# A fused gradient kernel on one core: first branch loads in two parts, a row tile placed by hand, loads at the half change reordered, the last step's sums moved up

## The chip, the cores and the metric

The kernel runs on one core of a Trainium2 chip. The metric is the time of one execution on the device in microseconds (us), the median of several. A ratio is computed as the mean time of one kernel's fast runs over the mean of the other's fast runs in the same rounds, so it is not quite the ratio of the medians that stand beside it.

A profile is one execution, traced. Executions of one kernel lay up to 7 us apart (1928.34 to 1935.41 in one group). Each kernel was traced once; as far as the traces of kernels with the same start tell, such differences come from when transfers land in the first 60 us, and from whether the clock falls after a wait, but this is inferred. A wait in a trace is therefore read as a mechanism, and the time as a ratio with its interval.

## The reference

It is the gradient of a layer norm that feeds two branches: a long convolution with a four-tap shift (branch A) and a gated two-layer network (branch B). Cut to what matters:

```python
xn = _layernorm(A_q)                      # S = 2048 rows, D = 1024
# branch A: k_shift = four taps of k by shift_k; kv = k_shift * v
#           y = irfft(rfft(kv) * rfft(ssm_k)) + kv * ssm_D;   a = xn * y
# branch B: gate = relu(xn @ W_gate); h = gate * (xn @ W_up);  b = h @ W_down   (F = 3584)
out = A_q + a + b
# returned: out and the gradients of q, k, v, shift_k, ssm_k, ssm_D, W_gate, W_up, W_down
```

## The kernel before

The program text is written once, and its order on each engine is then set by priorities and by ties. `keep_in_program_order` ties an instruction to the one of the same engine that was emitted just before it. `now()` and `late()` set the priority of what follows; what is late and not tied is placed wherever the queue has nothing more urgent.

```python
class Pri:
    LATE = 100_000_000
    def now(self):
        self.n += 64
        self.tc.cur_priority = self.n
    def late(self):
        self.n += 64
        self.tc.cur_priority = self.n + self.LATE
...
    def load(self, out, in_):                      # branch A's loads
        self.pri.now()
        ins = self.nc.sync.dma_start(out=out, in_=in_)
        if self.pin:
            self.tc.keep_in_program_order(ins)
        else:
            self.pri.pin(ins)

    def store(self, out, in_):                     # branch A's stores
        self.pri.late()
        self.pri.pin(self.nc.sync.dma_start(out=out, in_=in_))
```

The four taps of the shift go through a small array in memory, `sk_d`: transposed on TensorE, copied by ScalarE, stored, and later loaded again, one copy for each partition (`skb`). In the kernel before:

```python
    def shift_rows(self):
        ...
        self.act(sk_t[:], ps[:])
        self.store(self.sk_d, sk_t[:])
...
        self.shift_rows()
        self.pin = True
        nx = self.loads_1(0)      # hn, gt, xt, sD
        self.loads_2(nx)          # kp, vt, skb
        self.pin = False
        yield 11000
```

Branch B is computed in 7 blocks of 512 columns, for two halves of 8 row tiles each. In the first block the row tiles come straight from the layer norm, which works in chunks (0 to 3 of one row tile, 4 and later of two). Per chunk, ScalarE makes two row sums, VectorE averages them, ScalarE takes a square root, VectorE scales. TensorE then flips the row tile (`pst_x`), VectorE copies it (`xnT`), and the products with the gate weights (`wg`, result `ps_g`), the up weights (`wu`, `ps_u`) and the down weights (`wdT` with `goT`, `ps_h`) follow. VectorE turns each `ps_u` into `ru` and so frees its accumulator. Branch A runs beside this in 8 groups of 128 columns. Its work is cut into steps, each with a piece for TensorE and a piece for the other engines; an empty step has none for TensorE.

```python
            for sp in range(0, HS, 2):
                self.pri.now()
                while len(gT) < min(sp + 6, HS):
                    gT.append(self.load_T(g, len(gT), "goT", HS + len(gT)))
                ...
                yield from grad(sp)
                if ahead:
                    with self.tc.issue_after(self.stored.ins):
                        load(6 + sp // 2)          # rows of the layer norm's chunk 6, 7, ...
```

At the half change the second half's `xnT` and `goT` are loaded by transposing transfers between the next weights. `while late` and `late` in the diff below concern these. The last step, per row tile, is the gradient through the layer norm:

```python
            for ob in range(2):                    # two halves of 512 columns
                ... 56 matmuls into ps ...
                V.tensor_tensor_reduce(out=gx[:, oc], in0=ps[:], in1=gy[:, oc], ... accum_out=m[:, ob:ob + 1])
                V.tensor_tensor_reduce(out=pr[:, oc], in0=gx[:, oc], in1=xn[:, oc], ... accum_out=m[:, 2 + ob:3 + ob])
            ... three small operations on m ...
            for ob in range(2):
                nc.scalar.activation(out=w[:, oc], in_=xn[:, oc], ... scale=m[:, 5:6], bias=m[:, 4:5])
                V.scalar_tensor_tensor(out=gx[:, oc], in0=gx[:, oc], scalar=rstd, in1=gt[:, oc], ...)   # multiply-add
                V.tensor_tensor(out=o1[:, oc], in0=gx[:, oc], in1=w[:, oc], op=ALU.add)
                nc.sync.dma_start(out=out1[rows, oc], in_=o1[:, oc])
```

## Time and profile before

| | kernel before |
|---|---|
| time, median of 3 | 1940.89 us (1940.74 to 1941.39) |
| TensorE busy | 1891.5 us, 98% of the span |
| TensorE idle, 0 to 120 us | 16.4 us |
| granted clock of TensorE, 100 to 120 us | 0.83 |
| granted clock, 20 to 40, 40 to 60 and 120 to 140 us | 1.00 |

TensorE is the bound, so only its waits count, plus the stretches in which it ran at a lower clock. The prediction shows the lines.

### The profile page before, as it was taken

Reading aid. Unit: us, or ns where it says so; the run is one execution under the profiler, and the core shown is the slowest. Engines: PE = TensorE matmul, PEld = TensorE weight load, DVE = VectorE, ACT = ScalarE, POOL = GpSimd, SP = SyncE. Lnnn points to the kernel's source line nnn. Section 1 sums busy time; section 2 is a strip of 40 time slices with the busy share of each in tenths; the row PEclk is TensorE's granted clock in tenths of the full one; section 3 lists DMA queues with packets and bytes.
Section 4 is the critical chain, followed back from the end, with each engine's and each line's share of the span. In section 5 each row is a group of like instructions: output and inputs, shape, how many; then the busy total and the mean of one; then the engine's idle time right before and its main releaser. Section 6 shows DMA issues by size and latency. Waiting matters only on the chain.

```text
span 1938.3 us, 35924 instructions
## 1 busy us (share of the span) xinstructions
PE 1891.5 (98%) x15294; PEld 881.5 (45%) x15526; DVE 910.2 (47%) x1378; ACT 630.3 (33%) x863; POOL 15.3 (1%) x38
## 2 busy tenths in 40 slices
PE   8989999999999999999999999999999999999998
PEld 3434444444444444444444444444444444444443
DVE  6677777777686664444444344310122222222222
ACT  5555355355455444344344344311000000000000
POOL 1000000000000000000000000000000000000000
PEclk9999999999999999999999999999999999999999
DMA  9794887985775883654753643384999854554451
GB/s 252 233 196 131 179 186 172 212 200 131 180 186 132 217 244 107 151 149 141 197 148 106 145 123 121 99 233 178 259 238 245 204 134 121 120 121 122 118 121 36
DMA packets 616017, 319.08 MB, mean 165 GB/s; under 512 B 450984, under 2 KB 585136, under 8 KB 615856
## 3 DMA queue, kind: packets, MB, share of 16 engines
q1 hardware_dynamic: 605360, 295.79, 62.1%
q10 hardware_dynamic: 9216, 16.78, 2.8%
q0 software_dynamic: 1280, 4.20, 0.7%
q8 instruction: 121, 1.98, 0.4%
q14 instruction: 40, 0.33, 0.1%
HBM read 141.56 MB, written 95.44 MB: 122 GB/s over the span
## 4 chain that ended last, share of the span: by engine, by line
PE 66%; issue 2%; DMA 0%; DVE 0%; ACT 0%
PE ps_w L1032 19%; PE ps_x L1214 19%; PE ps_o L1180 10%; PE ps_d L1032 8%; PE ps L72 4%; PE ps_h L795 1%; PE ps_u L795 1%; PE ps_d L1045 1%; PE ps_g L795 1%; PE ps_w L1045 1%; DMA ugs<-ug_d 0%; PE pst L304 0%; DMA xn_nat<-xn_d 0%; DVE flp L315 0%; DVE o L1230 0%
## 5 line engine op out<-in xcount | busy, mean ns | idle before, releaser
L1032 PE MATMUL ps_w<-ugs,xn_nat 128*128 128x512 bf16 x1672 | 376.6, 379 | 5.3 <-issue 3.5
L795 PEld LDWEIGHTS <-xnT 128*128 128x128 bf16 x1792 | 170.5, 98 | 222.9 <-issue 13.0
L1032 PEld LDWEIGHTS <-xn_nat 128*128 128x128 bf16 x1728 | 165.0, 98 | 199.3 <-issue 5.5
L795 PE MATMUL ps_g<-wg,xnT 128*128 128x512 bf16 x868 | 205.6, 382 | 15.9 <-DMA wg<-in_B_W_gate_dram 9.3
L1227 ACT ACTIVATE w<-xn,m 128x512 f32<-128x512 bf16 x32 | 24.3, 806 | 559.5 <-issue 317.2
L795 PE MATMUL ps_h<-wdT,goT 128*128 128x512 bf16 x863 | 202.9, 379 | 3.3 <-issue 1.3
L795 PE MATMUL ps_u<-wu,xnT 128*128 128x512 bf16 x867 | 203.3, 379 | 2.3 <-issue 1.3
L1214 PE MATMUL ps_x<-wuT,guT 128*128 128x512 bf16 x879 | 197.6, 379 | 0.9
L1214 PE MATMUL ps_x<-wgT,ggT 128*128 128x512 bf16 x878 | 197.3, 379 | 0.9
L1180 PE MATMUL ps_o<-wd,hT 128*128 128x512 bf16 x878 | 192.6, 379 | 0.9
L1032 PE MATMUL ps_d<-g_nat,hs 128*128 128x512 bf16 x740 | 167.7, 379 | 3.3 <-issue 2.7
L1180 PEld LDWEIGHTS <-hT 128*128 128x128 bf16 x896 | 87.7, 98 | 105.7
L1214 PEld LDWEIGHTS <-guT 128*128 128x128 bf16 x896 | 87.7, 98 | 105.7
L1214 PEld LDWEIGHTS <-ggT 128*128 128x128 bf16 x896 | 87.7, 98 | 105.7
L895 DVE SCALAR_TENSOR_TENSOR ru<-ru,ps_u 128x512 bf16<-128x512 bf16 x112 | 76.6, 684 | 120.9 <-issue 48.6
L315 DVE STREAM_TRANSPOSE flp<-C 128x1024 f32<-128x1024 f32 x48 | 90.6, 1933 | 89.2 <-ACT C L76 89.2
L795 PEld LDWEIGHTS <-goT 128*128 128x128 bf16 x896 | 85.2, 98 | 103.3 <-issue 3.7
L1216 DVE CUSTOM_DVE_ANT_0 gx<-ps_x,gy 128x512 f32<-128x512 f32 x32 | 22.1, 692 | 215.2 <-PE ps_x L1214 205.4
L952 ACT CAST gh<-ps_h 128x512 bf16<-128x512 f32 x112 | 65.6, 585 | 169.6 <-PE ps_h L795 158.7
L76 ACT CAST C<-ps 128x1024 bf16<-128x1024 f32 x96 | 92.5, 1015 | 74.4 <-PE ps L72 73.4
L1130 ACT CAST wi<-ps_w 128x512 bf16<-128x512 f32 x108 | 63.7, 590 | 154.7 <-PE ps_w L1032 150.0
L315 DVE STREAM_TRANSPOSE flp<-B 128x1024 f32<-128x1024 f32 x48 | 90.8, 1938 | 47.8 <-ACT B L76 47.8
(169 smaller groups left out, 1517.3 us busy)
## 6 DMA issues: line engine op xcount, KB each, us to landing
ug_d<-ru SPq DMA_DIRECT2D x112, 256.0 KB, 3.3
ugs<-ug_d SPq DMA_DIRECT2D x112, 256.0 KB, 4.4
wg<-in_B_W_gate_dram SPq DMA_DIRECT2D x56, 256.0 KB, 4.3
wu<-in_B_W_up_dram SPq DMA_DIRECT2D x56, 256.0 KB, 5.8
h_d<-ht SPq DMA_DIRECT2D x112, 128.0 KB, 4.2
hs<-h_d SPq DMA_DIRECT2D x56, 256.0 KB, 5.1
out_dram<-wi SPq DMA_DIRECT2D x56, 256.0 KB, 2.8
gt<-in_grad_out_dram SPq DMA_DIRECT2D x32, 256.0 KB, 4.2
```

The lines of the kernel that those rows point to most:

```text
L72: self.pri.pin(self.nc.tensor.matmul(out, lhsT=lhsT, rhs=rhs, start=start, stop=stop))
L76: self.pri.pin(self.nc.scalar.copy(out=out, in_=in_))
L315: self.pri.pin(self.nc.vector.transpose(out=df[:, c0:c0 + 32, :], in_=sf[:, c0:c0 + 32, :]))
L795: self.pri.pin(self.nc.tensor.matmul(ps[:], lhsT=xT[:, kt * P:(kt + 1) * P], rhs=w(kt), start=(kt == 0), stop=(kt == self.DT - 1)), always ...
L895: self.pri.pin(nc.vector.scalar_tensor_tensor(out=ru[s][:, 1, :], in0=ru[s][:, 0, :], scalar=0.0, in1=ps[:], op0=ALU.is_gt, op1=ALU.mult))
L952: self.pri.pin(nc.scalar.copy(out=gh[:], in_=ps[:]))
L1032: self.pri.pin(self.nc.tensor.matmul(ps[:], lhsT=lhsT(st), rhs=rhs(st), start=(st == 0), stop=(st == self.ST - 1)))
L1045: self.pri.pin(self.nc.tensor.matmul(ps[i][:], lhsT=lhsT(i, st), rhs=rhs(i, st), start=(st == 0), stop=(st == self.ST - 1)))
L1130: self.pri.pin(nc.scalar.copy(out=wo[0][:, d, :], in_=ps[:]))
L1180: nc.tensor.matmul(ps[:], lhsT=hT[:, kt, :], rhs=self.wd[:, kt, oc], start=(kt == 0), stop=(kt == self.FT - 1))
L1214: nc.tensor.matmul(ps[:], lhsT=T[:, kt, :], rhs=W[:, kt, oc], start=(i == 0), stop=(i == n - 1))
L1227: nc.scalar.activation(out=w[:, oc], in_=xn[:, oc], func=ACT.Identity, scale=m[:, 5:6], bias=m[:, 4:5])
```

## The change

Its intent, part by part: (1) issue those of the branch's first loads that depend on nothing earlier, so that the gate weights of the third block are not stuck behind them; (2) take chunk 4 of the layer norm out of the way of the fourth row tile; (3) put two transposing loads of the half change behind the weights; (4) in the last step, make the small sums before the second multiply-add; (5) move one empty step ahead of the second transform of K. The core of the diff:

```diff
@@ loads_1, loads_2: xt (reads xn_d) and skb (reads sk_d) leave them
-        xt = self.xp.tile([P, 16, P], BF16, name="xt")
-        self.load_time(xt, self.xn_d, cg)
+    def load_xn(self, st):  ...
+    def load_taps(self, st):  ...
@@ start of the branch
-        self.shift_rows()
         self.pin = True
         nx = self.loads_1(0)
         self.loads_2(nx)
+        yield 12000
+        self.shift_rows()
+        yield 11000
+        self.load_xn(nx)
+        self.load_taps(nx)
         self.pin = False
-        yield 11000
+        yield 9000
...
-A_START = 66_000
+A_START = 45_000
@@ second transform of K
         yield None, q
+        yield None, q
         f2K = self.fwd2(st, "K", "fK")
         yield f2K, q
         yield None, q
         yield f2K, q
-        yield None, q
@@ first block of branch B: chunk 4
+                if sp == 2:
+                    chunk()
                 up(sp)
...
                 yield from first_gate_up(0)
-                chunk()
                 yield from first_gate_up(2)
@@ half change
                 if end:
                     load_up()
+                while end and late:
+                    late.pop(0)()
...
-                            ngT.append(self.load_T(g, HS + s, "goT", HS + s))
+                            late.append(lambda s=s: ngT.append(self.load_T(g, HS + s, "goT", HS + s)))
+                    while late and sp != HS - 4:
+                        late.pop(0)()
@@ last step: the first half's multiply-add at once, the three small operations tied, then
             for ob in range(2):
                 nc.scalar.activation(out=w[:, oc], ...)
+                if ob:
+                    hd(V.scalar_tensor_tensor(out=gx[:, oc], ...))
                 V.tensor_tensor(out=o1[:, oc], in0=gx[:, oc], in1=w[:, oc], op=ALU.add)
```

More of the change, by code (lines that the diff above doesn't have):

```diff
@@ L260, in loads_1, with load_xn @@
         self.load_time(gt, self.g, cg)
-        xt = self.xp.tile([P, 16, P], BF16, name="xt")
-        self.load_time(xt, self.xn_d, cg)
         sD = self.sm.tile([P, P], BF16, name="sD")
         self.load(sD[:], self.ssm_D[cg].partition_broadcast(P))
-        return dict(gi=gi, cg=cg, hn=hn, gt=gt, xt=xt, sD=sD)
+        return dict(gi=gi, cg=cg, hn=hn, gt=gt, sD=sD)
+    def load_xn(self, st):
+        xt = st["xt"] = self.xp.tile([P, 16, P], BF16, name="xt")
+        self.load_time(xt, self.xn_d, st["cg"])
     def gate_grad(self, st):
@@ L280, in loads_2, with load_taps @@
         self.load_time(vt, self.v, cg)
-        skb = self.sm.tile([P, 4, 1, P], BF16, name="skb")
+        st["kp"], st["vt"] = kp, vt
+    def load_taps(self, st):
+        skb = st["skb"] = self.sm.tile([P, 4, 1, P], BF16, name="skb")
         self.load(skb[:].rearrange("p i o c -> p (i o c)"),
                   self.sk_d[4 * st["gi"]:4 * st["gi"] + 4, :].rearrange("i c -> (i c)").partition_broadcast(P))
-        st["kp"], st["vt"], st["skb"] = kp, vt, skb
     def taps(self, st, out, src, offs):
@@ L499, in next_1 @@
                 st["nx"] = self.loads_1(gi + 1)
+                self.load_xn(st["nx"])
         def next_2():
@@ L503, in next_2 @@
                 self.loads_2(st["nx"])
+                self.load_taps(st["nx"])
         def next_gate():
@@ L858, in hidden @@
             nb = (n + 1) % self.FB
-            ru, nw = {}, [None, None, None]
+            ru, nw, late = {}, [None, None, None], []
             def load_gate():
@@ L1219, in grad_x @@
                                        op0=ALU.mult, op1=ALU.add, accum_out=m[:, 2 + ob:3 + ob])
-            V.tensor_tensor(out=m[:, 4:6], in0=m[:, 0:4].rearrange("p (a b) -> p a b", b=2)[:, :, 0],
-                            in1=m[:, 0:4].rearrange("p (a b) -> p a b", b=2)[:, :, 1], op=ALU.add)
-            V.tensor_scalar(out=m[:, 6:8], in0=m[:, 4:6], scalar1=-1.0 / D, scalar2=None, op0=ALU.mult)
-            V.tensor_scalar(out=m[:, 4:6], in0=m[:, 6:8], scalar1=self.rstd[:, st:st + 1], scalar2=None, op0=ALU.mult)
+                if ob == 0:
+                    self.tc.keep_in_program_order(V.scalar_tensor_tensor(
+                        out=gx[:, oc], in0=gx[:, oc], scalar=self.rstd[:, st:st + 1], in1=gt[:, oc], op0=ALU.mult,
+                        op1=ALU.add))
+            hd = self.tc.keep_in_program_order
+            hd(V.tensor_tensor(out=m[:, 4:6], in0=m[:, 0:4].rearrange("p (a b) -> p a b", b=2)[:, :, 0],
+                               in1=m[:, 0:4].rearrange("p (a b) -> p a b", b=2)[:, :, 1], op=ALU.add))
+            hd(V.tensor_scalar(out=m[:, 6:8], in0=m[:, 4:6], scalar1=-1.0 / D, scalar2=None, op0=ALU.mult))
+            hd(V.tensor_scalar(out=m[:, 4:6], in0=m[:, 6:8], scalar1=self.rstd[:, st:st + 1], scalar2=None,
+                               op0=ALU.mult))
             o1 = p_ev.tile([P, D], BF16, name="o1")
@@ L1227, in grad_x @@
                 nc.scalar.activation(out=w[:, oc], in_=xn[:, oc], func=ACT.Identity, scale=m[:, 5:6], bias=m[:, 4:5])
-                V.scalar_tensor_tensor(out=gx[:, oc], in0=gx[:, oc], scalar=self.rstd[:, st:st + 1], in1=gt[:, oc],
-                                       op0=ALU.mult, op1=ALU.add)
+                if ob:
+                    hd(V.scalar_tensor_tensor(out=gx[:, oc], in0=gx[:, oc], scalar=self.rstd[:, st:st + 1],
+                                              in1=gt[:, oc], op0=ALU.mult, op1=ALU.add))
                 V.tensor_tensor(out=o1[:, oc], in0=gx[:, oc], in1=w[:, oc], op=ALU.add)
```

## The prediction

> **What bounds the kernel now.** I read, in this order, the busy times of the page, the busy time per stretch of the span, the list of waits of TensorE, and then the timelines around the few waits that it names.
>
> ```profile
> PE 1891.5 (98%) x15294; PEld 881.5 (45%) x15526; DVE 910.2 (47%) x1378; ACT 630.3 (33%) x863; POOL 15.3 (1%) x38
> ```
>
> TensorE (PE) is the bound: 1938.3 - 1891.5 = 46.8 us is all that it does not work. The change removes no matmul, so it can only give back part of these 46.8 us plus what a throttled clock costs. Faster by 2% would need 38.8 us. The view by stretches says where the idle time is: 16.4 us in the first 120 us (4.6 of them between 20 and 40, 8.1 between 100 and 120), 2.5 us between 320 and 360, 7.5 us after 1900, and otherwise 0.3 to 2 us per 100 us. The list of TensorE's waits (total us, times, longest) gives the early ones names:
>
> ```profile
> PE ps_g L795 <- DMA wg<-in_B_W_gate_dram: 9.3, 3, 7.3
> PE ps_g L795 <- DVE xnT L827: 3.9, 3, 2.9
> ...
> PE pst_x L824 <- DVE ln_x L776: 1.8, 2, 1.6
> ...
> PE ps L72 <- DVE flp L315: 1.5, 3, 0.8
> ```
>
> In the timeline of TensorE (start, length, what, and in brackets the idle time before it with its releaser) the single cases are:
>
> ```profile
> 22.18 0.62 PE L824 MATMUL pst_x<-ident,ln_x 128*128 128x128 bf16 x8 [1.63 <-DVE ln_x L776]
> ...
> 27.39 1.90 PE L795 MATMUL ps_g<-wg,xnT 128*128 128x512 bf16 x8 [2.87 <-DVE xnT L827]
> ...
> 113.96 3.59 PE L795 MATMUL ps_g<-wg,xnT 128*128 128x512 bf16 x8 [7.30 <-DMA wg<-in_B_W_gate_dram]
> ...
> 357.39 1.24 PE L795 MATMUL ps_g<-wg,xnT 128*128 128x512 bf16 x4 [0.53 <-DMA wg<-in_B_W_gate_dram]
> 360.06 3.03 PE L795 MATMUL ps_g<-wg,xnT 128*128 128x512 bf16 x12 [1.43 <-DMA wg<-in_B_W_gate_dram]
> ```
>
> The longest is explained by the sync queue's own timeline before it. The queue issues in order, and it stood still from 91.7 to 98.1 us:
>
> ```profile
> 90.31 1.42 SPq L88 DMA_DIRECT2D gt<-in_grad_out_dram  x2
> 98.12 1.31 SPq L88 DMA_DIRECT2D xt<-xn_d  x2
> 99.48 1.19 SPq L88 DMA_DIRECT2D sD<-in_A_ssm_D_dram  x1
> 100.72 3.60 SPq L88 DMA_DIRECT2D kp<-in_A_k_dram  x4
> 104.36 1.83 SPq L88 DMA_DIRECT2D vt<-in_A_v_dram  x2
> 106.24 1.58 SPq L88 DMA_DIRECT2D skb<-sk_d  x1
> ...
> 108.39 1.26 SPq L957 DMA_DIRECT2D ug_d<-ru  x2
> 109.74 2.22 SPq L788 DMA_DIRECT2D wg<-in_B_W_gate_dram  x4
> ```
>
> The load of xt reads xn_d, whose last rows GpSimd stores at 91.9 to 93.0; they land some 5 us later (5.0 us is the median landing of these stores). Behind it sD, kp, vt and skb take 8.3 us of issuing, and only then come the gate weights that TensorE wants at 106.66. At the very end of the kernel, the timeline of VectorE and ScalarE shows the last row tile:
>
> ```profile
> 1932.09 0.16 DVE L1220 TENSOR_TENSOR m<-m 128x2 f32<-128x2 f32 x1
> 1932.17 0.74 DVE L1228 SCALAR_TENSOR_TENSOR gx<-gx,rstd,gt 128x512 f32<-128x512 f32 x1
> 1932.83 0.16 DVE L1222 TENSOR_SCALAR m<-m 128x2 f32<-128x2 f32 x1
> 1933.03 0.23 DVE L1223 TENSOR_SCALAR m<-m,rstd 128x2 f32<-128x2 f32 x1
> 1933.34 1.52 ACT L1227 ACTIVATE w<-xn,m 128x512 f32<-128x512 bf16 x2 [22.66 <-issue]
> ```
>
> A 0.74 us multiply-add stands between the small sums that the activation waits for.
>
> **What the Trainium skill says.** First, "TensorE: Matmul & The Clock Gate", section "What's actually happening": after an idle window of about 3.4 us the clock falls to half until TensorE has been busy for such a window. The trace agrees: after the 7.30 us wait the granted clock from 113.96 to 117.35 is 0.50, and these matmuls last up to 634 ns where the group's median is 379. Second, the same page, section "Architectural detail": VectorE and ScalarE take their instructions strictly in order. The trace fits: the copy of xnT that TensorE waited for at 27.39 ran on VectorE at 26.66, directly behind the layer norm of a later chunk. Third, "Perfetto Trace Analysis", section "DMA Instruction — HWDGE (DVE, Sync)": an issuing sequencer first waits for the semaphore, then holds the descriptor generator, and only then takes the next instruction. That is the standstill before xt at 98.12. Fourth, "DMA: Bandwidth & Descriptors", section "Issuing engines are not separate DMA queues": all transfers share 16 engines. It matters for the first 60 us, where the trace's DMA share is 1.03 to 1.06.
>
> **The change part by part.**
>
> Part 1, loads in two parts. hn, gt, sD, kp and vt move about 12 TensorE steps (12 x 1.73 = 21 us) earlier, to about 65 us; xt and skb stay near 90; the start of the branch does not move (66 + 11 against 45 + 12 + 11 + 9, both 77 in the pacing's units). The last xn_d store does not get later, so xt is issued at 98.1 again (every time here is on the old scale), skb at 99.4, the two ug_d stores at 101.1, and wg at about 102.4: 7.3 us sooner. In the old trace TensorE began 113.96 - 109.74 = 4.2 us after the first wg issue; 102.4 + 4.2 = 106.6, and TensorE wants it at 106.66. So the 7.30 us wait goes nearly whole. I keep 0.3 us, as four tiles issued over 2.2 us may trail. The throttle goes with it: from 113.96 to 118.20 the clock was half, so 4.24 / 2 = 2.1 us, plus 0.1 us at the next group (2.02 against 1.89). Sum: 7.3 + 2.2 - 0.3 = **9.2 us**. Can VectorE follow? In the new order the branch's gate product starts when it did (104.7), and the taps follow at about 106.9 in place of 111.75; the flip is then done at about 118.6, where the second transform is reached at 130.07 - 9.2 = 120.9. It holds, with some 2 us left.
>
> Part 2, the fourth row tile. Taking chunk 4 of the layer norm out of the way of chunk 3: between 18.5 and 21.6 VectorE did 1.3 us of chunk 4's work, and ScalarE's square root waited for a row sum (1.04 us). I put the fourth tile at 21.3 instead of 22.18, so TensorE's 1.63 us wait shrinks by about 0.9; its copy then comes right behind, at about 22.7, before the multiply by up-weights ends at 23.6, so the 2.87 us wait vanishes. Gain to there: about 3.8 us. But chunk 4 now starts its sums at about 21, where it was 17.8, and took 8 us; its tiles are ready at 29 to 30, and TensorE, running 3.8 us ahead, wants them at 32.58 - 3.8 = 28.8. I give back 0.8 us: **3.0 us**. Chunk 5 (done at 39.5) is wanted at 43.93 - 3.0 = 40.9, fine.
>
> Part 3, the half change. In the old queue two goT transposes were issued at 348.86 and held it for 4.31 us; the gate weights went out at 353.94. Their buffer was free when the last gate product ended, at about 348.6. With the transposes behind both weights, wg goes out some 4 to 5 us sooner, and 0.53 + 1.43 = **2.0 us** go. The late tiles are used over 20 us later.
>
> Part 4, the last step. Without the 0.74 us instruction, the two small ones follow 0.2 us apart and the activation starts at about 1932.8 in place of 1933.34: **0.5 us**. In the other 15 row tiles VectorE is idle 7 to 10 us per half, so there it is worth nothing.
>
> Part 5, one empty step moved before the second transform of K, in each of eight groups. The wait for the flip arose three times, 0.78 + 0.34 + 0.42 = 1.5 us, and a step is 1.7 us long, so it should go. The product that reads K has one step less; VectorE waits there, but has had idle steps behind. I count **1.2 us**.
>
> Sum: 9.2 + 3.0 + 2.0 + 0.5 + 1.2 = 15.9 us. 1940.9 - 15.9 = 1925.0; I add 0.5 us for small new waits and predict **1925.5 us**, a ratio of 0.992.
>
> **The rivals.**
>
> A: the wait moves. xn_d still bounds xt, and xt still stands ahead of the weights. If the stores land later (their landing runs up to 8.2 us), or if the earlier 2 MB of loads push the stores and weight transposes of the stage at 65 to 75 us back, then wg comes 2 to 4 us later than I say. For it: the standstill of 6.4 us remains in the queue. Against it: hn and gt no longer fly beside the last xn_d store, and from 70 to 90 the DMA share is only 0.35 to 0.53. Result: 1928 to 1930, or up to 1932 when the wait passes 3.4 us and throttles again.
>
> B: the start is bound by transfers. The DMA share is over 1 until 60 us, so a TensorE that runs 3 us ahead might meet inputs not landed (goT, the weights of the second block). Against it: in the old trace TensorE has no wait for a DMA there; the second block's gate weights were issued at 52.0 to 54.7 and wanted at 61.5. Result: part 2 worth 0 to 1 us, 1927.5 to 1928.5.
>
> C: everything goes, chunk 4 is ready in time too: 9.5 + 4.5 + 2.0 + 0.5 + 1.5 = 18.0, so 1923.
>
> **Range and chances.** C is nearly the floor, 1922.5 with rounding; A in its bad form with a part of B sets the upper end, 1932. Faster by 2% would be under 1902, which 46.8 us of idle time, most of it in start, end and gaps of 0.16 us, cannot give. Slower by 2% would take a race of waits that no part introduces; all transfers moved are moved earlier, or behind something more urgent.
>
> **What would show it.** Right: the wait for wg near 106 us gone or under 1 us and the clock 1.00 from 100 to 120; wg issued straight behind xt, skb and two ug_d stores; no wait for xnT at the fourth tile, and one of about 1 us at the fifth; no wg wait at the half change; the last activation 2.2 us after the last product's first sum starts, where it was 2.7 (1930.62 to 1933.34). Wrong: a wait of over 2 us for wg in front of the third block, a new wait on goT or wdT before 60 us, or TensorE waiting for VectorE in the first group of the branch.

## More of the kernel before

The kernel before was run again beside each group of experiments; its medians lie between 1939.95 and 1941.35 us, so every experiment is read by its ratio to the runs of before of its own group.

The sync queue's timeline (start, time in the queue, line, transfer, count) has the store of the taps well before anybody wants them:

```profile
88.97 0.34 SPq L96 DMA_DIRECT2D sk_d<-sk_t  x1
```

## The result, and the profile after

The changed kernel took 1938.76 us (median of 4, 1937.82 to 1940.31) beside 1940.82 us (median of 4) of the kernel before. The ratio is 0.999, with a 95% interval of 0.9972 to 1.0007: the same within 2%, as foretold, but the gain is about 2 us where 15.4 were predicted, and the time is outside the range.

The list of waits of TensorE after (total us, times, longest us) has lost the wait for the gate weights, 9.3 us before, and has got others:

```profile
PE pst_x L834 <- DVE ln_x L786: 5.5, 3, 4.5
...
PE ps L72 <- DVE flp L319: 3.2, 1, 3.2
...
PE ps_h L805 <- DMA wdT<-in_B_W_down_dram: 1.4, 1, 1.4
...
PE ps_d L1060 <- ACT wo L1112: 0.8, 1, 0.8
```

In the timeline of TensorE after (idle time and its releaser in brackets):

```profile
33.92 1.30 PE L834 MATMUL pst_x<-ident,ln_x 128*128 128x128 bf16 x16 [4.54 <-DVE ln_x L786]
...
108.67 1.89 PE L805 MATMUL ps_g<-wg,xnT 128*128 128x512 bf16 x8
...
122.50 1.89 PE L805 MATMUL ps_g<-wg,xnT 128*128 128x512 bf16 x8 [1.59 <-DVE ru L905]
127.61 1.06 PE L72 MATMUL ps<-flp,FW 64*32 64x128 bf16 x64 [3.23 <-DVE flp L319]
...
145.60 0.60 PE L72 MATMUL ps<-kvt,R 64*128 64x512 bf16 x4
...
366.05 0.59 PE L805 MATMUL ps_h<-wdT,goT 128*128 128x512 bf16 x2 [1.42 <-DMA wdT<-in_B_W_down_dram]
```

The third block's gate product starts at 108.67 with no wait, where it started at 113.96 after 7.30 us: 5.3 us ahead. But by 127.61 TensorE has waited 1.59 + 3.23 us for VectorE, and the throttle follows: the view by stretches gives a granted clock of 0.83 between 120 and 140, where before it had 0.83 between 100 and 120. The product on kvt, which reads what the taps produce, starts at 145.60. In the kernel before:

```profile
145.30 0.60 PE L72 MATMUL ps<-kvt,R 64*128 64x512 bf16 x4
```

So all of the lead is gone within 37 us. Every later row of the comparison is small. Cut at three milestones of TensorE's timeline (differences of starts; the last column is the span; `ps_d` holds products of the gradient of W_down, `ps_o` those of branch B's output):

| kernel | to kvt | kvt to first ps_d | ps_d to first ps_o | ps_o to the end | span |
|---|---|---|---|---|---|
| before | 145.30 | 548.00 | 656.96 | 588.04 | 1938.3 |
| after | 145.60 | 545.41 | 658.11 | 588.28 | 1937.4 |

The first column holds parts 1 and 2, the second parts 3 and 5, the third another piece of part 5, and the last part 4. Three of the four columns are longer after the change.

**Where the lead went.** The sync queue's timeline after:

```profile
97.27 1.37 SPq L88 DMA_DIRECT2D xt<-xn_d  x2
...
100.34 2.40 SPq L798 DMA_DIRECT2D wg<-in_B_W_gate_dram  x4
...
109.51 0.59 SPq L96 DMA_DIRECT2D sk_d<-sk_t  x1
113.03 0.33 SPq L88 DMA_DIRECT2D skb<-sk_d  x1
```

The gate weights are issued at 100.34, even earlier than the 102.4 of the prediction. But the store of the taps, issued at 88.97 before, is now issued at 109.51, although ScalarE had made `sk_t` at 80.12; and `skb`, which the prediction put at 99.4, has to wait for it until 113.03. The cause stands in the two program texts. The store is late by priority. In the kernel before, the next instruction of its queue was a pinned load, and a pin ties the load to the store: the store could go no later than the load. The change moved the loads ahead of `shift_rows`, so nothing follows the store that is tied to it, and it sank behind everything urgent. VectorE's timeline after shows the price:

```profile
115.94 1.23 DVE L80 TENSOR_TENSOR ksh<-kp,skb 128x2048 bf16<-128x2048 bf16 x1 [6.92 <-DMA skb<-sk_d]
```

In the kernel before this first tap started at 111.75. All taps, the multiplies that free the accumulators (`ru`) and the flip (`flp`) are in one engine's order, and so TensorE waited for two of them.

**The start.** ScalarE's timeline after:

```profile
30.91 1.06 ACT L742 ACTIVATE ln_j<-ln_x 128x1024 bf16<-128x1024 bf16 x1 [3.44 <-DMA ln_x<-in_A_q_dram]
...
31.96 0.19 ACT L774 ACTIVATE ln_s<-ln_s 128x2 f32<-128x2 f32 x1
```

The 0.19 us square root of chunk 4 stands behind the first row sum of chunk 5 (VectorE had its input ready at 27.60), and that sum waits for chunk 5's rows to land. In the kernel before the same root ran ahead of that sum, at 23.90:

```profile
23.90 0.20 ACT L764 ACTIVATE ln_s<-ln_s 128x2 f32<-128x2 f32 x1 [0.65 <-DVE ln_s L763]
```

The fourth row tile gained nearly what was foretold (the gate product behind it starts at 24.04 in place of 27.39, with no wait), and the fifth lost it: a wait of 4.54 us, and a clock of 0.91 from 20 to 40. The second block's first gate product starts at 63.30, where it was 61.52 before.

**The half change.** The gate weights are issued at 349.62 in place of 353.94 and nothing waits for them. But the displaced transposes, of which two hold the queue for 4.54 us, still stand ahead of the last piece of the down weights:

```profile
355.20 4.54 SPq L822 DMA_TRANSPOSE goT<-in_grad_out_dram  x2
```

That piece goes out at 362.49, where it went out at 363.87 before: 1.4 us sooner. TensorE begins the product that needs it at 363.18 in place of 366.38, 3.2 us sooner, and so it now waits 1.42 us inside it.

**The last step.** VectorE's timeline of the last row tile after:

```profile
1932.50 0.69 DVE L1252 TENSOR_TENSOR o<-gx,w 128x512 bf16<-128x512 f32 x1 [0.93 <-ACT w L1248]
1933.11 0.75 DVE L1250 SCALAR_TENSOR_TENSOR gx<-gx,rstd,gt 128x512 f32<-128x512 f32 x1
1933.96 0.69 DVE L1252 TENSOR_TENSOR o<-gx,w 128x512 bf16<-128x512 f32 x1
```

In the kernel before, the lines that the prediction shows were followed by both output sums at once:

```profile
1934.18 1.40 DVE L1230 TENSOR_TENSOR o<-gx,w 128x512 bf16<-128x512 f32 x2 [0.93 <-ACT w L1227]
```

The multiply-add did not vanish; it moved from ahead of the activation to between the two output sums. From the start of the last product's first sum (1930.62 before, 1929.48 after) to the end of the last output sum it took 1935.58 - 1930.62 = 4.96 us before and 1934.65 - 1929.48 = 5.17 after.

### The profile page after: what moved, and what is told of

The parts are those of the page before. It is cut to its first block, busy times and chain, and to the rows that moved or that the text cites. A ratio compares the mean times of both kernels' runs of the same rounds, so it can differ in the third digit from the quotient of the medians.

```text
span 1937.4 us, 35957 instructions
## 1 busy us (share of the span) xinstructions
PE 1893.5 (98%) x15294; PEld 883.2 (46%) x15526; DVE 910.9 (47%) x1378; ACT 629.9 (33%) x863; POOL 15.6 (1%) x38
## 4 chain that ended last, share of the span: by engine, by line
PE 91%; issue 3%; DMA 2%; SPq 1%; DVE 1%; ACT 1%; ACTq 0%; DVEq 0%; POOLq 0%
PE ps_w L1047 19%; PE ps_x L1229 19%; PE ps_o L1195 10%; PE ps_h L805 9%; PE ps_g L805 9%; PE ps_u L805 9%; PE ps_d L1047 8%; PE ps L72 7%; PE ps_d L1060 1%; SPq L822 1%; PE ps_w L1060 1%; DMA ln_x<-in_A_q_dram 1%; DMA wg<-in_B_W_gate_dram 1%; SPq L816 0%; PE pst L308 0%
```

## The experiments

15 kernels, all correct. The first eight test the two causes named above, the next four measure part 1 by itself and carry the best version on, and the last three settle parts 4 and 5.

### The store put back

This is the changed kernel with:

```diff
         self.act(sk_t[:], ps[:])
-        self.store(self.sk_d, sk_t[:])
+        self.pri.now()
+        self.tc.keep_in_program_order(self.nc.sync.dma_start(out=self.sk_d, in_=sk_t[:]))
```

> The changed kernel with one instruction tied to its place: the store of sk_d stays directly behind the copy that makes sk_t (80 us), ahead of the load of xt, where the changed kernel issues it at 109.5. Theory 1 (the late store keeps skb from landing until 115.9, so the taps and behind them the flip come late): skb is issued right behind xt at about 98.7, the first tap runs by 109, the two waits of TensorE for VectorE near 122 to 127 (1.59 and 3.23 us) go, the clock is 1.00 from 120 to 140, and the products on kvt start at about 138 in place of 145.6: 7.7 us less in the end, about 1931.1 us. Rival (VectorE is too full in the first group: 19.1 us busy of 20 from 120 to 140): the flip stays late by 2 to 4 us even with skb there, and the gain is 2 to 4 us. Rival (what is saved here is taken back by a later transfer): no gain at the end although the products on kvt start early.

Measured: 1930.79 us (1927.72 to 1931.66) beside 1941.35, ratio 0.9945 (0.9931 to 0.9958). This is the first theory's 1931.1 us. The waits on the flip and on `ru` are gone, the clock is 1.00 from 120 to 140, and the product on kvt starts 8.8 us earlier than after. TensorE's timeline of this run:

```profile
136.84 0.60 PE L72 MATMUL ps<-kvt,R 64*128 64x512 bf16 x4
```

One store, a tie and a priority are worth more than the whole change had brought. The fifth row tile's wait (4.02) and the wait for `wdT` (1.4) are still there.

### The root ahead of chunk 5's sums, alone and with the store

The first is the changed kernel with a tie that keeps chunk 5's first sums on ScalarE behind chunk 4's square root; the second has the same tie on top of the store.

```diff
+                if i == 5:
+                    with self.tc.issue_after(self.root4.ins):
+                        total = row_sums(j, 0, ACT.Copy)
```

> The changed kernel with one order tied on ScalarE: the square root of layer norm chunk 4 before the first row sum of chunk 5. Theory 1 (the root stood behind a sum that waits for its transfer until 30.9): the fifth row tile's wait of 4.54 us falls to 0 to 1 us, the clock stays 1.00 from 20 to 40 (was 0.91), the second block starts at 57 to 58 in place of 63.3, and about 5.5 us reach the end: 1933.3 us. Rival (the start is bound by transfers): a wait of about the same size turns up before 60 us on goT, wdT, the sixth to eighth row tiles or the second block's weights, and the second block starts at 61 or later; 1937 to 1939 us.

> Both ties together. Theory 1, with the two losses independent: 1938.8 - 7.7 - 5.5 = 1925.6 us, which is what the prediction had for the whole change. If one loss only hides the other (the start's gain is waited away at the load of xt, whose source lands at a time set by transfers), the sum is not reached: 1930 us or more.

Measured: 1937.96 us (1933.36 to 1938.08), ratio 0.9979 (0.9967 to 0.9992), and with the store 1931.01 us (1930.24 to 1932.28), ratio 0.995 (0.9937 to 0.9962). The theory's 1933.3 and 1925.6 were missed; with the store, the tie gains nothing over the store alone (0.9945). The traced execution of the first was by far its shortest, at 1933.36; the others took 1937.45 to 1938.08. In it chunk 5's rows were there at 28.4, and the clock stayed at 1.00 from 120 to 140 although TensorE waited 3.22 us for the flip. VectorE's timeline of the run with both shows what replaces the wait:

```profile
32.68 0.17 DVE L757 TENSOR_SCALAR ln_b<-ln_s 128x2 bf16<-128x2 f32 x1 [2.31 <-ACT ln_j L743]
...
34.55 1.28 DVE L844 COPY xnT<-pst_x 128x1024 bf16<-128x1024 bf16 x2
```

The row tile is flipped early (a wait of 0.76 us), but its copy stands on VectorE behind chunk 5's average, which waits for ScalarE's sum, which waits for the same transfer. TensorE waits 2.46 us for `xnT`. The order on ScalarE was one way by which the late transfer reached TensorE; the order on VectorE is a second.

### Parts 3, 4 and 5 without 1 and 2

The kernel before with the half change, the last step and the moved empty step.

> The kernel before with the half change, the last step and the moved empty step alone, without the two-part loads and without the moved row tile. My sum for these three was 2.0 + 0.5 + 1.2 = 3.7 us, 1937.1 us. The trace of the changed kernel shows a new wait of 1.42 us for wdT behind the half change; with it 2.3 us, 1938.5 us. Rival (the moved empty step makes VectorE late elsewhere): no gain, or a new wait of TensorE for VectorE in every group.

Measured: 1939.10 us (1938.27 to 1942.37), ratio 0.9993 (0.9981 to 1.0006). The wait for the third block's gate weights stays (7.6), the three small waits on the flip of K are gone, a wait of 1.3 us for `wdT` is there. The 3.7 us predicted for these three parts would be a ratio of 0.9981, the very edge of the interval; the middle is 1.4 us, and the 2.3 us that the expectation had with the wait for `wdT` fit. So they probably gave less than predicted.

### Chunk 5 loaded earlier, the transposes behind the down weights, and the tie as well

All three stand on top of the store. First, chunk 5's rows ahead of the first four transposes of `goT`; second, in addition, the displaced `goT` transposes of the half change behind the down weights; third, the first with the tie of the root.

```diff
+    load(5)
     goT = [b.load_T(g, i, "goT", 8 + i) for i in range(4)]
-    load(5)
```

```diff
-                while end and late:
-                    late.pop(0)()
...
                     load_down(sp // 2)
+                    while sp == HS - 2 and late:
+                        late.pop(0)()
```

> The kernel of e1 (store of sk_d in its place) with the rows of layer norm chunk 5 loaded ahead of the four goT transposes instead of behind them; the order on ScalarE and VectorE is left as it is, with the root of chunk 4 behind the first sum of chunk 5. Theory 2 (the fifth row tile waits for chunk 5's transfer, which lands at 28.4 to 30.9 because it is issued behind eight transposes; the order on ScalarE, or on VectorE when the root is freed, only hands that wait on): the load is issued at about 18.5, the first sum of chunk 5 no longer waits for it, the fifth tile's wait falls from 4.0 to about 1.2 us, the clock from 20 to 40 is 1.00, the second block starts at about 58.5 in place of 62.3: 1926.4 us against 1930.8 of e1. Rival (the transposes delayed by the load, or transfers as a whole, bound the start): a wait for goT or wdT of 2 us or more before 40 us, no gain over e1.

> e5_load_early, and at the half change the late goT transposes go behind the last wdT piece as well. If the 1.4 to 2.3 us wait of TensorE for wdT there is the two transposes in front of it in the queue (4.5 to 5 us of issuing), it vanishes: 1.5 us less than e5, about 1924.9 us. Rival (wdT lands late because all transfers are slow there): the wait stays above 1 us and the time is that of e5.

> e5_load_early with the order on ScalarE tied too (root of chunk 4 first). Theory 2: both are out of the way, the fifth tile's wait is under 0.8 us and no new wait of 2 us for xnT as in e3 appears: 0.5 us less than e5, about 1925.9 us. If the order on ScalarE were the cause by itself, e7 would be about 3 us faster than e5.

Measured, beside 1939.95 us: 1932.76 (1928.34 to 1935.41), ratio 0.9956; 1927.32 (1926.17 to 1933.25), ratio 0.9936 (0.9924 to 0.9948); 1932.40 (1930.41 to 1934.28), ratio 0.9958. The second confirms the half change: no wait there, and its ratio is 0.002 under that of the first, some 4 us. The two intervals overlap slightly (the first has 0.9944 to 0.9968), and the traces show 2.0 us of it (545.74 and 543.74 in the second column). The early load alone was a miss: the fifth row tile's wait fell to 0.98 us and the clock from 20 to 40 to 1.00, yet the time is no better than that of the store alone (0.9945). Its trace is of its shortest execution, 1928.34; what held the longer ones was not traced. The tie on top of it changes nothing (0.9958 beside 0.9956); had the order on ScalarE been the cause by itself, it should have brought about 3 us. TensorE's timeline of the third run has a new wait:

```profile
47.76 0.59 PE L812 MATMUL ps_h<-wdT,goT 128*128 128x512 bf16 x1 [5.65 <-DVE ru L912]
```

And ScalarE's timeline of that run, just before:

```profile
43.60 1.06 ACT L743 ACTIVATE ln_j<-ln_x 128x1024 bf16<-128x1024 bf16 x1 [6.93 <-DMA ln_x<-in_A_q_dram]
```

Now it is chunk 6 that has not landed: its load is issued at 37.32 in this run, behind four more transposes (28.69 to 36.11). ScalarE waits 6.93 us for it, VectorE stands behind ScalarE with an average ahead of `ru`, and TensorE waits 5.65 us for an accumulator. The lead is handed on to the next chunk and lost there. In the second run the same wait was 2.65 us.

### The fourth row tile put back

The store in place, part 2 undone.

> The kernel of e1 without the moved chunk (the layer norm chunk 4 back ahead of the second pair of row tiles). What the moved row tile is worth as it stands: I had 3.0 us. The traces of before and e1 put the second block at 61.5 and 62.3, so by theory 2 it is worth nothing or costs up to 1 us: 1930.0 us here against 1930.8 of e1. If it is worth 3 us, this run takes 1934.

Measured: 1932.03 us (1929.92 to 1932.94), ratio 0.9952 (0.994 to 0.9964), beside 0.9945 of the store with part 2. Part 2 is not seen in the time. The waits at the start are as in the kernel before (1.63 at 22.41, 2.87 at 27.62), and the second block's first gate product starts at 61.95; with part 2 it started at 62.34, and in the kernel before at 61.52. These are three ways through the start, and they arrive within 1 us. TensorE's timeline at the half change of this run:

```profile
357.73 0.59 PE L806 MATMUL ps_h<-wdT,goT 128*128 128x512 bf16 x2 [2.04 <-DMA wdT<-in_B_W_down_dram]
358.25 1.08 PE L72 MATMUL ps<-GH,IA 32*64 32x128 bf16 x64
```

The wait for `wdT` was 2.04 us, and the product after it took 1.08 us where its like takes 0.76. The granted clock is 0.83 from 355 to 365, which costs 10 x 0.17 = 1.7 us on top.

### Part 1 alone, without and with the store

These are the kernel before with part 1, and the same with the store in place.

> The kernel before with part 1 alone (loads in two parts). Theory: the early gate weights bring about 8 us at the third block, and the displaced sk_d store gives them back through late taps (a wait on the flip, half clock until about 134), so the products on kvt start where they did (145 to 146) and the time is within 2 us of the kernel before. Rival: part 1 is itself worth little, and the gain seen at the third block comes from parts 2 and 3: then there is no store wait worth 6 us and the wait for wg stays at several us.

> The kernel before with part 1 alone, and the sk_d store put in place. Theory: 8 to 9 us faster than the kernel before, ratio about 0.9955; the wait for wg before the third block is gone, there is no wait on the flip over 1 us, and the products on kvt start 8 to 9 us earlier than in the kernel before (about 137). Rival: as part 1 alone, within 2 us of it.

Measured, beside 1941.35: 1937.99 us, ratio 0.9989 (0.9976 to 1.0003), and 1931.92 us, ratio 0.9954 (0.9941 to 0.9966). In the first, the waits for the gate weights are down to 1.1 us in all, the store is issued at 107.97, `skb` at 111.51, and TensorE waits 1.70 us for `ru` and 3.22 us for the flip. The product on kvt starts at 142.72, somewhat earlier than I had said. In the second the waits for `ru` and for this flip are gone and kvt starts at 136.86. So part 1 is worth 1941.35 x 0.0046 = 8.9 us (6.6 to 11.5) with its store and about 2 us without it, which the interval does not tell from nothing.

### The best version without part 2 and the early load, and with chunk 6 early as well

First, the store, parts 1, 3, 4 and 5 and the transposes behind the down weights. Second, the best version so far with:

```diff
                 self.pri.now()
+                if ahead and sp == 0:
+                    load(6)
                 while len(gT) < min(sp + 6, HS):
                     gT.append(self.load_T(g, len(gT), "goT", HS + len(gT)))
```

> The kernel after with the store in place, without part 2, chunk 5's load where it was, and the late goT transposes behind the down weights as in the best version. Theory, that neither part 2 nor the early load is worth anything: the same as the best version, ratio 0.9936 to 0.994 (some 12 us under the kernel before), and the wait for wdT at the half change gone. Rival, that the early start is worth its 2 to 3 us: 0.995 or more.

> The best version so far with chunk 6's load of the layer norm ahead of the second set of goT transposes as well. Theory, that the chain of the start is bound by when each chunk's rows land: chunk 6's load is issued at about 27 us in place of 35.8, ScalarE's sum waits no longer, the 2.65 us wait before ps_h near 45 us goes, the second block starts at about 58 in place of 60.8, and the ratio falls to about 0.992. Rival: the wait moves on to the transposes of goT or the weights that are now later, or to chunk 7, and the ratio stays at 0.9936.

Measured: 1928.18 us (1928.05 to 1929.62), ratio 0.9935 (0.9923 to 0.9947), and 1925.64 us (1925.24 to 1927.78), ratio 0.9923 (0.9911 to 0.9936). The first says that part 2 and chunk 5's early load, together, are worth nothing that shows (0.9936 with them). In the second, chunk 6's load is issued at 28.49, ScalarE waits for no rows between 28 and 50 us, and the wait before `ps_h` near 45 us is gone. TensorE's timeline has one again, one chunk later:

```profile
58.66 1.89 PE L806 MATMUL ps_h<-wdT,goT 128*128 128x512 bf16 x8 [2.24 <-DVE ru L906]
```

The chain is the same as for chunks 5 and 6, now with chunk 7, whose load was issued at 48.83. ScalarE's timeline of that run:

```profile
54.51 1.06 ACT L743 ACTIVATE ln_j<-ln_x 128x1024 bf16<-128x1024 bf16 x1 [3.77 <-DMA ln_x<-in_A_q_dram]
```

VectorE's average of these sums, at 56.73, stands ahead of `ru`, at 57.93. The second block starts at 60.42, where 58 was expected and the best version so far had 60.76. The kvt product starts at 134.93, where it started at 135.49 in that version and at 134.65 in the trace with the early load of chunk 5 alone. So the theory is confirmed for chunk 6, and the rival named where the wait went: most of each gain at the start is handed on. The intervals of the two runs of this section overlap, so the 2.5 us between them are not shown beyond doubt.

### Parts 4 and 5

The first is part 5 alone on the kernel before; then comes the best version with the second half's multiply-add put directly behind the small sums, and with the old order of part 5 in the last group of the branch; then the same with the old order in the sixth group instead.

```diff
             hd(V.tensor_scalar(out=m[:, 4:6], ...))
+            hd(V.scalar_tensor_tensor(out=gx[:, 512:], in0=gx[:, 512:], scalar=..., in1=gt[:, 512:], ...))
...
                 nc.scalar.activation(out=w[:, oc], ...)
-                if ob:
-                    hd(V.scalar_tensor_tensor(out=gx[:, oc], ...))
```

> The kernel before with part 5 alone (the empty step moved before the second transform of K). Theory: the three waits on the flip (0.78, 0.34 and 0.42 us) go, and a new wait for ScalarE's copy of wo, 0.8 us, appears near 902 us in the last group, because the copy of K now stands ahead of that copy on ScalarE: net some 0.7 us in the trace. Rival, as predicted: no new wait, net 1.2 us or more. The time itself moves by less than the runs can resolve.

> The best version (chunk 6 early), with the second half's multiply-add put directly behind the small sums, ahead of the output sums, and with the old order of the steps in the last group alone. Theory: in the last row tile the multiply-add fills VectorE's 0.9 us wait for the activation, and from the start of the last product's first sum to the end of the last output sum it takes 4.4 us, where it was 4.96 in the kernel before and 5.17 after; the wait for wo (0.84 us) near 890 us is gone; span some 1.5 us under chunk 6 early, 1923.5. Rival: the multiply-add delays the first output sum, so the end stays at 5.0 us or more; and the old order brings its own wait back (a wait on the flip in the last group).

> The best version with the mended last step, and the old order of the empty step in the sixth group, where the wait for wo stands (the run before had it in the eighth, where it changes nothing). Theory: the wait for wo near 890 us is gone and no other comes in its place, for the kernel before had none in this group; the stretch from the first ps_d product to the first ps_o product is 0.8 to 1.1 us shorter than in the mended run (there 658.0); the time itself, about 1 us less, is within what the runs scatter, ratio 0.992. Rival: a wait on the flip of K comes back in this group, and the stretch stays.

Measured: 1940.36 us beside 1940.42, ratio 0.9998 (0.9985 to 1.0012); 1926.48 us (1924.64 to 1927.08), ratio 0.9923 (0.991 to 0.9937); 1924.97 us (1923.79 to 1927.6) beside 1940.82, ratio 0.992 (0.9906 to 0.9933). Part 5 alone takes the three waits on the flip away and brings the wait of 0.84 us for `wo`, at 904.26. VectorE's timeline of the mended last row tile:

```profile
1919.98 0.74 DVE L1252 SCALAR_TENSOR_TENSOR gx<-gx,rstd,gt 128x512 f32<-128x512 f32 x1
1921.00 1.40 DVE L1258 TENSOR_TENSOR o<-gx,w 128x512 bf16<-128x512 f32 x2 [0.28 <-ACT w L1257]
```

The multiply-add fills what was a wait of 0.93 us for the activation. From the first sum at 1917.98 to 1922.40 it takes 4.42 us, as expected: 0.54 less than before and 0.75 less than after. The other half of that run's edit failed: the wait for `wo` stayed, because it stands in the sixth group and the edit was made in the last. With the old order in the sixth group it is gone.

The same milestones, for the runs that the next section rests on:

| kernel | to kvt | kvt to first ps_d | ps_d to first ps_o | ps_o to the end | span |
|---|---|---|---|---|---|
| part 1 alone | 142.72 | 547.25 | 657.01 | 588.12 | 1935.1 |
| part 1 and store | 136.86 | 548.06 | 657.12 | 588.06 | 1930.1 |
| parts 3 to 5 | 145.14 | 545.13 | 657.94 | 588.29 | 1936.5 |
| part 5 alone | 147.61 | 546.08 | 657.91 | 588.10 | 1939.7 |
| chunk 6 early | 134.93 | 543.92 | 657.91 | 588.24 | 1925.0 |
| last step mended, old order in the sixth group | 135.06 | 543.62 | 656.96 | 587.56 | 1923.2 |

The last row is the best version: it beats the kernel before by 0.8% and the changed one by about 0.7% (0.992 over 0.999). It is also the only one of these rows that is better than before in every column but the third, where it is equal.

The third and the fourth column repeat closely over all 17 traced kernels, so they carry parts 4 and 5 better than the times do. In the third, the four kernels with the old order in the sixth group have 656.96 to 657.12, the other 13 have 657.88 to 658.11. In the fourth, the four kernels without part 4 have 588.04 to 588.12, the eleven with part 4 as it was made 588.24 to 588.33, and the two with the mended last step 587.56 and 587.58.

## Why the prediction was right or wrong

The class was right: no part could bring 2%. The time was wrong. The sum promised 15.9 us, 15.4 with the allowance for new waits; 2 came. By the sizes below, some 7 of the missing 13 us were lost in part 1, 3 in part 2, 1 in part 3 and 0.7 in part 4 (an estimate from single runs and traces).

**Part 1, 9.2 us.** The mechanism and the size were right for the stretch that the prediction looked at: `wg` early, the 7.30 us wait gone, the clock 1.00 from 100 to 120. Part 1 with its store measured 8.9 us. The step that failed is "skb at 99.4". It took for granted that the load of the taps follows `xt` at once. It reads `sk_d`, and the prediction asked when `xn_d` is stored and never when `sk_d` is. The store's place in the queue had hung on the load behind it, and the change took that load away. From there on, "the taps follow at about 106.9" became 115.94, "with some 2 us left" became a lack, and the wait for weights was replaced by a wait for VectorE of 1.59 + 3.23 us and the half clock behind it. None of the three rivals had that wait, although the last sentence of the prediction named TensorE waiting for VectorE in the first group of the branch as what would make it wrong. The run with the store (107.44 for the first tap, the flip done at 119.80, TensorE there at 121.60) shows that the rest of this step's reckoning holds. (The 5.0 us that it gives as the median landing of the `xn_d` stores is 5.3 on the page; `xt` was issued when it said all the same.)

**Part 2, 3.0 us.** Up to the fourth row tile the working held. The step that failed is "its tiles are ready at 29 to 30" for chunk 4, with only 0.8 us to give back. It took chunk 4's own work, moved it by 3 us, and left out that the same engine now has chunk 5's sum between chunk 4's sums and its square root, and that this sum waits for a transfer. The Trainium skill's page "TensorE: Matmul & The Clock Gate", section "Architectural detail", which the prediction had cited for just this, says that ScalarE and VectorE take their work in strict order; the trace agrees, with the root at 31.96 behind a sum that waited 3.44 us. Rival B, the start bound by transfers, was the right one, and its 0 to 1 us for this part fit, as far as the times resolve them. Its wording was too narrow, though: TensorE has no wait for a transfer there. It waits for VectorE, which waits for ScalarE, which waits for the transfer. That is shown by five runs in which freeing one link moved the wait to the next: chunk 5's rows by way of the copy of `xnT` (2.46 us), chunk 6's rows by way of `ru` (1.37, 2.65 and 5.65), and chunk 7's by way of `ru` (2.24).

**Part 3, 2.0 us.** The gate weights came 4.3 us sooner and 1.96 us of waits went, as foretold. The step that failed is "The late tiles are used over 20 us later", which is beside the point: it asked when the moved transfers are wanted, not what is queued behind them. Behind them was the last piece of `wdT`, and TensorE waited 1.2 to 2.3 us for it in all eight traces with this order. Parts 3 to 5 and part 5 alone differ by 546.08 - 545.13 = 0.95 us in the second column: that is part 3 as it was made, in one pair of traces. With the transposes behind all weights, the run without part 2 gained another 0.0017 in ratio (0.9952 to 0.9935; the intervals overlap), and in the second column 547.31 - 543.56 = 3.75 us, which waits of 2.04 + 0.22 us and 1.7 us of clock account for. All five traces with that order have 543.56 to 543.92 there, 2.2 to 2.5 us under part 5 alone: about the 2.0 us of the prediction.

**Part 4, 0.5 us.** The activation did start 0.54 us earlier (2.18 in place of 2.72 us after the first sum). The step that failed is "Without the 0.74 us instruction": it was followed to the activation and not to the end of the kernel. There the displaced instruction costs its 0.75 us again, so the part lost 0.2 us (the fourth column, in every trace). In its other place, in the wait for the activation, it gave the 0.5 us.

**Part 5, 1.2 us.** It was right in size by luck: two errors cancel. The second column gained 1.9 us (548.00 to 546.08), more than the 1.54 us of the three waits; the third lost 0.95, because ScalarE's copy of K then came ahead of its copy of `wo`, and TensorE waited 0.84 us for an accumulator. "VectorE waits there, but has had idle steps behind" looked at the one engine that was not concerned. The net is about 1 us. The loss in the third column repeats in all 13 traces with this order; the gain in the second is from one trace, and the times do not resolve the net (0.9985 to 1.0012).

**What stays open.** Part 2 was not measured by itself on the kernel before, only by taking it out of two versions; there the ratio rose by 0.0007 (1.4 us) in the one and fell by 0.0001 in the other, with intervals of some 2.5 us to either side. Nor is it settled how much of the last 2.5 us, from chunk 6's early load, is real, or why the early load of chunk 5 alone did not show in the time.

## What to carry to other kernels

When instructions are moved, look at what they had held in place: a late store that is ordered only by its neighbour drifts when the neighbour leaves, and then everything that reads it is late. Follow every displaced piece of work to the end of the chain (what stands behind it in its new queue, on each in-order engine), not only to the wait that it left. And where a chain of in-order engines starts with a transfer, as in a kernel's first microseconds, move the transfer; changing the order of one engine hands the wait to the next.

## What the Trainium skill lacked or had wrong

- "TensorE: Matmul & The Clock Gate", section "What's actually happening", has the clock fall after an idle window of about 3.4 us, and says that the window runs freely. The runs show a lower clock after shorter waits, and not always: after 2.04 us at 357.73 in the run without part 2 the clock was 0.83 from 355 to 365, and after 2.65 us at 44.84 in the run with the transposes behind the down weights it was 1.00 from 40 to 60. One and the same wait, 2.86 or 2.87 us at 27 us, left the clock from 20 to 40 at 1.00 in three traced kernels (before, parts 3 to 5, part 5 alone) and at 0.91 in four (those with part 1 and without part 2). So a wait of 2.0 to 3.2 us may or may not be charged a second time; none of 1.2 to 1.8 us that stood alone was here.
- No page gives the time for which a transposing load of this size holds the issuing queue on this chip; the one count that was found, in "DMA: Bandwidth & Descriptors", is for small tiles and stands in a table about trn3. Here four loads of `goT` (256 KB each) took 5.7 to 9.4 us of the sync queue in the first 40 us, waits included, and four plain loads of the same size (`wg`, `wu`) 2.0 to 3.5 us between 45 and 120 us. The runs that changed the order around them show that this is what made chunk 5, chunk 6 and the last piece of `wdT` late.
- "Perfetto Trace Analysis", section "DMA Instruction — HWDGE (DVE, Sync)", explains a queue that stands still before one transfer, and the trace agrees (6.4 us before `xt` in the kernel before). It has nothing on a transfer that is issued late because the program's scheduler placed it so: the queue's list of waits has none for the store at 109.51, although `sk_t` was made at 80.12, and its cause is found only by comparing the order of the two programs.
